# Past the head of the kernel, scales cross the partitions by a DMA transpose of 16-bit powers of two in SBUF instead of a float32 transpose on TensorE

## The chip, the cores and the metric

The kernel runs on one core of a Trainium2 chip. Five engines work from their own in-order queues: TensorE (PE, with its weight loads PEld), VectorE (DVE), ScalarE (ACT), GpSimd (POOL) and SyncE (SP), the last of which here does nothing but issue DMAs. The metric is the device time of one execution in microseconds (us); lower is better.

## The reference

Two independent parts are computed and set side by side. Part A is causal sliding-window attention with 32 heads of 32 columns and a window of 256; part B is a Fourier mixing layer as matrix products.

```python
# A: x [2048, 1024], wqkv [1024, 3072], wo [1024, 1024]
qkv = (x @ wqkv).reshape(B, S, 3, H, Dh)            # H = 32, Dh = 32
scores = einsum("bhqd,bhkd->bhqk", q, k) * Dh ** -0.5
mask = (i - j >= 0) & (i - j < 256)
a = softmax(where(mask, scores, -1e9)) @ v  ->  [S, D] @ wo
# B: x [2048, 1024], sequence DFT [2048, 2048] and hidden DFT [1024, 1024], real and imaginary
p = x @ hid_re.T ; r = x @ hid_im.T
b = seq_re @ p - seq_im @ r
out = concatenate([a, b], axis=-1)                   # [1, 2048, 2048] float32
```

## The kernel before, in words

Every large product runs in float16 on TensorE with each operand split into a high and a low part (`PASSES`: high by high, high by low, low by high). So each float32 piece has to be scaled into float16's range first. The scale is a power of two taken from the largest value of the whole piece (or, where ScalarE measures it, from the sums of absolute values of each partition). Three steps make it:

- `top` (VectorE) or `mean` and `u_top` (ScalarE, output `junk`) leave one number per partition;
- `spread` reduces these to one column `[128, 1]`, called `top_u`, `top_wk` and so on;
- `scale_of` brings the 128 numbers of that column to every partition. Before the change TensorE transposes the column, broadcast to 128x128, against the identity `ident` into a PSUM tile `pt_...`; VectorE takes the maximum along each row of `pt`, masks its exponent, clamps it and takes the reciprocal.

The program has three stages. In the **head** (steps 0 to 10 of `order`) inputs arrive and the first scales are made. In the **projection stage** (96 steps; q, k and v of the heads, 24 matmuls of 512 columns each) a step `at(n, ...)` emits the loads, scales and splits that later steps need. In the **unit stage** 48 units follow: for each half of the DFT, 4 units of kind `x` (part B's first product) and 8 units of kind `c` (its second product). A unit is seven sub-products of 12 matmuls (function `seven`), at positions 0 to 6 in three PSUM banks in the order a, b, a, c, a, b, a. At position 4 bank a is added into the output tile by VectorE (`y<-p_a`, line 1035), at position 5 bank b is (`y<-p_b`). Position 6 accumulates into bank a again, so it can't begin before the add of position 4 has read the bank.

Attention (`attention`) is a generator that `tick` advances in small steps between the matmuls of both stages. Its blocks need VectorE (masking `s`, maximum `mx`, low part `hl`, sum `o`), ScalarE, GpSimd and a DMA transpose from SP for each block (`t<-hl`, 128x512 or 128x1024 of float16) and one for each four blocks (`ot<-ohl`, 128x512).

For a unit of kind `c` the hooks are, counted from its own number n: load its two raw pieces `raw_u` in unit n - 3, measure them (`u_top`) at positions 0 and 2 of unit n - 2, `u_scale` at position 6 of unit n - 2, split (`un_a`, `un_b`, `un_c`) in unit n - 1. This is only the order in which the code is written. A list scheduler with its own model of each operation's time decides in which order each engine's queue holds the instructions, within what data and explicit `issue_after` edges allow.

Of the kernel before, what the change touches and what calls it, by code (L numbers as in the profile page):

```python
# [9 lines left out]
F32 = mybir.dt.float32  # L10
F32R = mybir.dt.float32r
F16 = mybir.dt.float16
BF16 = mybir.dt.bfloat16
U8 = mybir.dt.uint8
U32 = mybir.dt.uint32
AF = mybir.ActivationFunctionType
ALU = mybir.AluOpType
AX = mybir.AxisListType

P = 128  # L20
S = 2048
D = 1024
H = 32
# [5 lines left out]
CH = 512  # L29
NCH = S // CH  # L30
QB = CH // P
VW = 2 * DH + 2
# [8 lines left out]
VW = 2 * DH + 2  # L41
# [12 lines left out]
def fused_kernel(ctx: ExitStack, tc: tile.TileContext, xa, wqk, wv, wo, xb, wd, cs, out):  # L54
    nc = tc.nc
# [8 lines left out]
    const = ctx.enter_context(tc.tile_pool(name="const", bufs=1))  # L64
# [4 lines left out]
    ps_v = ctx.enter_context(tc.tile_pool(name="ps_v", bufs=1, space=PSUM))  # L69
# [8 lines left out]
    tsum = reg1[:, :7 * 8 * CH].rearrange("p (s h k c) -> p s h k c", s=7, h=2, k=4)  # L78
    spare = reg1[:, 7 * 8 * CH:]

    ident = const.tile([P, P], F32, name="ident")
    make_identity(nc, ident)


    upper = const.tile([P, P], F32, name="upper")
# [2 lines left out]
                            fill=0.0, base=0, pattern=[[1, P]], channel_multiplier=-1)  # L88
    upper2 = upper.bitcast(U32).unsqueeze(1).to_broadcast([P, 2, P])
    never = const.tile([P, 1], F32, name="never")  # L90
# [3 lines left out]
    pshift = const.tile([P, 1], F32, name="pshift")  # L94
    nc.gpsimd.memset(pshift, PSHIFT)

    nbank, units_on = [0], []

    def bank(name):
        nbank[0] += 1  # L100
        return ps_m.tile([P, CH], F32, tag=f"m{nbank[0] % 3}", name=name)
# [6 lines left out]

    junk = const.tile([P, ND * P], U8, name="junk")
    fixed = []  # L110
# [8 lines left out]
    def vec(f, *args, **kwargs):  # L119
        with tc.issue_after(latest[0].ins) if strict[0] and latest else nullcontext():  # L120
            latest[:] = [f(*args, **kwargs)]  # L121
        return latest[0]
# [10 lines left out]
        return const.tile([P, 2], F32, name=f"sc_{name}")  # L133

    tops, head = {}, [True]


    behind = []
# [18 lines left out]
    def spread(key, n):  # L157
        t = tops.pop(key)
        if n > 1:
            t1 = small.tile([P, 1], F32, tag="top0", name=f"top1_{key}")  # L160
            vec(nc.vector.tensor_reduce, t1, t, axis=AX.X, op=ALU.max)
        else:
            t1 = t
        tops[key] = t1

    def scale_of(key, v, s, down=2.0 ** -14):

        if head[0]:
            pt = ps_s.tile([P, CH], F32, tag="s", name=f"pt_{key}")[:, :P]
            with tc.issue_after(fixed[0].ins) if fixed else nullcontext():  # L170
                fixed[:] = [nc.tensor.transpose(pt, tops.pop(key).to_broadcast([P, P]), ident)]
        else:
            pt = (ps_v.tile([P, CH], F32, tag="pv", name=f"pt_{key}") if units_on else bank(f"pt_{key}"))[:, :P]
            nc.tensor.transpose(pt, tops.pop(key).to_broadcast([P, P]), ident)
        vec(nc.vector.tensor_reduce, v, pt, axis=AX.X, op=ALU.max)
        vec(nc.vector.tensor_scalar, v.bitcast(U32), v.bitcast(U32), 0x7F800000, None, op0=ALU.bitwise_and)
        vec(nc.vector.tensor_scalar, v, v, 2.0 ** -100, down, op0=ALU.max, op1=ALU.mult)
        vec(nc.vector.reciprocal, s, v)
# [218 lines left out]
    def at(n, f, *args):  # L397
        tasks.setdefault(n, []).append((f, args))
# [151 lines left out]
    for (kd, g), n in use.items():  # L550
        if kd in "qk" and n >= 4:
            at(n - 6, w_load, kd, g)
            at(n - 4, w_top, kd, g)
            at(n - 3, w_finish, kd, g)
    for g in range(NG):
        at(max(use["q", g], use["k", g], 11), scores_scale, g)

# [3 lines left out]
        at(n, x_split, 0, (i,), behind_act)  # L561
    at(7, strict.__setitem__, 0, False)
    at(7, head.__setitem__, 0, False)
    at(4, x_top, 2, (0, 1))
    at(5, x_top, 2, (2, 3))
    at(7, x_finish, 2)
# [4 lines left out]
    at(11, x_known)  # L571
    at(11, wv_load, 0)
    at(14, wv_top, 0)
    at(15, wv_scale, 0)
    for i, n in enumerate((15, 16, 16, 17)):
        at(n, wv_split, 0, (i,))
    at(15, wv_load, 1)
    at(18, wv_top, 1)
    at(19, wv_scale, 1)
    for i, n in enumerate((19, 20, 21, 21)):  # L580
        at(n, wv_split, 1, (i,))
    at(20, wv_known)
    def scan(key, ns):
# [292 lines left out]
    at(len(order) - 3, x_left, 0, "c")  # L876


    with tc.tile_pool(name="pa", bufs=2) as pa:
        def qk_out(kd, g, c, ps, f):  # L880
            y = pa.tile([P, 2, CH], F16, tag="yq", name=f"y{kd}{g}_{c}")
            behind_act[:] = [nc.scalar.activation(y[:, 0], ps, AF.Copy, scale=f)]
            behind[:] = [vec(nc.vector.scalar_tensor_tensor, y[:, 1], ps, f, y[:, 0],
                             op0=ALU.mult, op1=ALU.subtract)]
            a = "qk".index(kd)
            nc.sync.dma_start(qk[g, c, a:a + 2, :, :, a].rearrange("j d h t -> (d h) j t"), y)
            nc.sync.dma_start(qk[g, c, 2 - 2 * a, :, :, a].rearrange("d h t -> (d h) t"), y[:, 0])

        def d_out(g):
            qk_out("q", g, 0, direct.pop(g), f0[:, g:g + 1])  # L890

        w_top("q", 0)
        x_top(0, (0, 1, 2, 3))
        d_mm(0, range(0, 4))
        w_scale("q", 0)
        d_mm(0, range(4, 8))
        w_top("q", 1)
        d_mm(1, range(0, 1))
        x_scale(0)
        d_known(0)  # L900
        d_mm(1, range(1, 3))
        w_scale("q", 1)
        d_known(1)
        d_out(0)
        w_split("q", 0)
        w_top("q", 2)
        d_mm(1, range(3, 8))
        x_top(1, (0, 1))
        d_out(1)
        d_mm(2, range(0, 2))  # L910
        w_scale("q", 2)
        d_known(2)
        x_top(1, (2, 3))
        d_mm(2, range(2, 8))
        w_top("q", 3)
        d_mm(3, range(0, 2))
        x_scale(1)
        x_split(1, (0, 1))
        d_out(2)
        d_mm(3, range(2, 4))  # L920
        w_scale("q", 3)
        d_known(3)
        x_split(1, (2,))
        d_mm(3, range(4, 8))
        x_split(1, (3,))
        w_split("q", 1)
        d_out(3)

        for n, (kd, g, c) in enumerate(order):
            if n < 4:  # L930
                continue
            if n == 22:
                first_cm.__exit__(None, None, None)
                att_cm = tc.tile_pool(name="att", bufs=2, side="right")
                cell["att"] = att_cm.__enter__()
                agen[0] = attention()
                upcoming[0] = next(agen[0])
            for f, args in tasks.pop(n, ()):
                f(*args)
            rate[0] = 2 * early * EARLY.get(n, 0.85) / 24  # L940
            ps = bank(f"p{kd}{g}_{c}")
            if kd == "v":
                t = c
                product(ps, lambda h, d: xin[:, t // 4, h, d, t % 4 * P:t % 4 * P + P],
                        lambda h, d: reg2[:, g, h, d])
                y = pa.tile([P, H // 2, VW], F16, tag="yv", name=f"yv{g}_{t}")
                nc.gpsimd.memset(y[:, :, DH:DH + 1], 1.0)
                nc.gpsimd.memset(y[:, :, 2 * DH + 1:], 0.0)
                f = vf[:, g, t // 4:t // 4 + 1]
                pv = ps.rearrange("p (h d) -> p h d", d=DH)  # L950
                behind_act[:] = [nc.scalar.activation(y[:, :, :DH], pv, AF.Copy, scale=f)]
                behind[:] = [nc.vector.scalar_tensor_tensor(y[:, :, DH + 1:2 * DH + 1], pv, f, y[:, :, :DH],
                                                            op0=ALU.mult, op1=ALU.subtract)]
                nc.sync.dma_start(vs[t, :, g * (H // 2) * VW:(g + 1) * (H // 2) * VW],
                                  y.rearrange("p h w -> p (h w)"))
            else:
                u = wun[kd, g]
                product(ps, lambda h, d: u[:, h, d], lambda h, d: xin[:, c, h, d])
                qk_out(kd, g, c, ps, DOWN if kd == "q" else kf[:, c:c + 1])
            if kd == "v" and g == 0 and c % 4 == 3:  # L960
                ready.add((0, c // 4))
            if kd == "v" and g == 1 and c == NT - 1:
                pass
            if kd == "k" and g > 0:
                ready.add((g, c))
# [116 lines left out]
            hook(pos)  # L1082


    units_on.append(True)
    perm, turns = [(nbank[0] + 1 + k) % 3 for k in range(3)], [0]
    with tc.tile_pool(name="pb", bufs=1) as pb:
        ybufs = [pb.tile([P, 2, CH], F32, name=f"y{k}") for k in range(3)]
        ybufs.append(spare[:, 16 * P:].bitcast(F32).rearrange("p (e c) -> p e c", e=2))
        ny = [0]  # L1090
# [11 lines left out]
        for r in range(4):  # L1102
            x0, c0 = 12 * r, 12 * r + 4
            for j in range(4):
                n = x0 + j
# [5 lines left out]
            for j in range(8):  # L1111
                n = c0 + j
# [20 lines left out]
        for n, (kind, p, c, i) in enumerate(units):  # L1133
# [35 lines left out]
            f = fu.pop(n)  # L1169
# [16 lines left out]
        for q in range(NT // 2):  # L1186
# [5 lines left out]
                  lambda t, y, at_=0: nc.sync.dma_start(out[t * P:t * P + P, at_:at_ + y.shape[1] * y.shape[2]],  # L1192
                                                        y.rearrange("p e c -> p (e c)")),
# [51 lines left out]
```

## Time and profile before

| what | us |
|---|---|
| runs of the kernel before, median of 3 | 1716.21 (1709.82 to 1716.93) |
| the profiled execution, whole | 1715.44 |
| its span, first to last instruction | 1713.7 |
| DVE busy in the span | 1302.1 |
| ACT busy | 1170.1 |
| POOL busy | 575.5 |

The profile gives, for each engine, busy time and the idle time ahead of a group of instructions with what ended it. A wait for several things is put down to the one that came last. Matmuls overlap one another, so the distance from one matmul's start to the next, not its duration, is what it takes of TensorE. The 1.7 us between span and whole execution lie outside the first and last instruction.

### The profile page before, as it was taken

The page shows a single profiled execution, that of the slowest core. Times are in us where ns is not written, and L with a number is a line of the kernel's source. Part 1 is how long each engine was busy: PE and PEld are TensorE (multiplying, and loading weights), DVE is VectorE, ACT ScalarE, POOL GpSimd, SP SyncE. Part 2 cuts the span into 40 slices and gives each one's busy share as a digit, 9 for nine tenths or more (in the row PEclk, how much of TensorE's full clock was granted, in tenths as well). Part 3 has the DMA queues.
Part 4 walks back from the last instruction along what each step waited for, and adds up shares of the span by engine and source line. Part 5 has one row for each costly group of instructions (what it writes and reads, how often), then busy time and mean ns, then how long its engine had stood idle before and what let it go on. Part 6 is the DMA issues. An engine that isn't in the chain of part 4 may idle for free.

```text
span 1713.7 us, 30874 instructions
## 1 busy us (share of the span) xinstructions
PE 1694.8 (99%) x10999; PEld 852.4 (50%) x10999; DVE 1302.1 (76%) x2225; ACT 1170.1 (68%) x2035; POOL 575.5 (34%) x874
## 2 busy tenths in 40 slices
PE   9999999999999999999999999999999989999999
PEld 4444555555555544555554555545545545444444
DVE  6847788887987788887688886698876698688442
ACT  4566666676877787887687886688876678563322
POOL 0001222344434441444423565434565424411000
PEclk9999999999999999999999999999999999999999
DMA  9747999999998994887998999987999986875431
GB/s 349 245 137 242 252 291 289 271 262 299 243 245 198 215 226 121 206 196 182 229 244 241 196 182 181 223 196 127 197 169 185 203 203 127 166 193 118 117 98 74
DMA packets 469899, 348.63 MB, mean 203 GB/s; under 512 B 376944, under 2 KB 409968, under 8 KB 468848
## 3 DMA queue, kind: packets, MB, share of 16 engines
q1 hardware_dynamic: 462064, 321.48, 74.7%
q0 software_dynamic: 7680, 25.17, 9.2%
q8 instruction: 86, 1.41, 0.4%
q14 instruction: 69, 0.57, 0.1%
HBM read 166.99 MB, written 106.17 MB: 159 GB/s over the span
## 4 chain that ended last, share of the span: by engine, by line
PE 84%; DMA 5%; DVE 4%; ACT 4%; issue 2%; POOL 1%; SPq 0%; ACTq 0%; DVEq 0%; POOLq 0%
PE p_a L114 23%; PE pv L114 14%; PE p_b L114 11%; PE pk L114 9%; PE pq L114 9%; PE p_c L114 6%; PE po_a L114 5%; PE s L114 3%; PE po_b L114 2%; DMA raw_u<-in_cs_dram 2%; DMA t<-hl 1%; PE far L114 1%; PE po_c L114 1%; ACT reg L833 1%; DVE raw_u L791 1%
## 5 line engine op out<-in xcount | busy, mean ns | idle before, releaser
L266 ACT ACTIVATE s<-s,bias,escs 128x256 f32<-128x256 f32 (+1 forms) x512 | 270.1, 528 | 11.7
L284 POOL TENSOR_SCALAR_AFFINE_SELECT z<-t 128x512 f16<-128x512 f16 x224 | 186.4, 840 | 180.4 <-PE pv L114 137.4
L270 DVE TENSOR_TENSOR hl<-s,hl 128x512 f16<-128x512 f32 (+1 forms) x256 | 169.9, 664 | 61.6 <-ACT hl L269 59.5
L259 ACT ACTIVATE bias<-mx,pshift,escs 128x2 f32<-128x2 f32 x256 | 98.2, 384 | 169.3 <-DVE mx L256 168.8
L114 PEld LDWEIGHTS <-reg 128*128 128x128 f16 x1344 | 129.1, 98 | 141.5
L286 POOL TENSOR_SCALAR_AFFINE_SELECT t<-t 128x512 f16<-128x512 f16 x224 | 183.9, 830 | 11.4
L114 PE MATMUL p_a<-reg,un_c 128*128 128x512 f16 x768 | 181.2, 379 | 1.8 <-ACT y L1033 1.3
L114 PE MATMUL pk<-reg,wu_k 128*128 128x512 f16 x768 | 174.4, 379 | 0.0
L256 DVE TENSOR_REDUCE mx<-s 128x2 f32<-128x512 f32 (+1 forms) x256 | 170.7, 667 | 3.4
L114 PE MATMUL pv<-reg,reg 128*128 128x512 f16 x768 | 172.7, 379 | 0.0
L114 PEld LDWEIGHTS <-un_c 128*128 128x128 f16 x1152 | 110.0, 97 | 124.0 <-issue 4.9
L114 PEld LDWEIGHTS <-un_b 128*128 128x128 f16 x1152 | 110.1, 97 | 123.9 <-issue 7.8
L263 POOL TENSOR_SCALAR mark<-bias 128x1 f32<-128x1 f32 x128 | 52.3, 409 | 355.2 <-ACT bias L259 355.0
L114 PEld LDWEIGHTS <-un_a 128*128 128x128 f16 x1152 | 109.8, 97 | 116.2
L269 ACT ACTIVATE hl<-s 128x512 f16<-128x512 f32 (+1 forms) x256 | 148.8, 581 | 13.6 <-DMA t<-hl 8.3
L114 PE MATMUL pq<-reg,wu_q 128*128 128x512 f16 x672 | 151.3, 379 | 0.8 <-DVE reg L121 0.5
L114 PE MATMUL p_a<-reg,un_b 128*128 128x512 f16 x576 | 136.4, 379 | 4.7 <-DVE y L1035 3.0
L114 PE MATMUL p_b<-reg,un_b 128*128 128x512 f16 x576 | 136.3, 379 | 1.2 <-ACT y L1033 1.0
L114 PE MATMUL p_a<-reg,un_a 128*128 128x512 f16 x576 | 136.6, 379 | 0.0
L114 PE MATMUL p_c<-reg,un_a 128*128 128x512 f16 x576 | 136.5, 379 | 0.0
L254 DVE COPY_PREDICATED s<-upper,far 128x256 f32<-128x256 uint32 x224 | 94.2, 420 | 46.0 <-PE s L114 45.0
L114 PEld LDWEIGHTS <-qk 96*128 96x128 f16 x1056 | 87.9, 97 | 64.1 <-DMA qk<-qk 1.9
(208 smaller groups left out, 3154.1 us busy)
## 6 DMA issues: line engine op xcount, KB each, us to landing
raw_u<-in_cs_dram SPq DMA_DIRECT2D x64, 512.0 KB, 4.9
qk<-qk SPq DMA_DIRECT2D x64, 384.0 KB, 5.1
out_dram<-y POOLq DMA_DIRECT2D x72, 256.0 KB, 6.3
raw_wd<-in_wd_dram SPq DMA_DIRECT2D x24, 512.0 KB, 5.3
vs<-yv SPq DMA_DIRECT2D x32, 264.0 KB, 4.2
vt<-vs SPq DMA_DIRECT2D x64, 132.0 KB, 4.2
raw_wo<-in_wo_dram SPq DMA_DIRECT2D x16, 512.0 KB, 9.2
qk<-yq SPq DMA_DIRECT2D x32, 256.0 KB, 3.1
```

Source lines behind the costliest of these rows:

```text
L114: fixed[:] = [nc.tensor.matmul(*args, **kwargs)]
L254: nc.vector.copy_predicated(s[:, :, P:], upper2, d["far"] if nb == 3 else never2)
L256: nc.vector.tensor_reduce(mx, sv, axis=AX.X, op=ALU.max, negate=True)
L259: nc.scalar.activation(bias, mx, AF.Identity, bias=pshift, scale=es)
L263: marks[:] = [nc.gpsimd.tensor_scalar(mark, bias[:, 0:1], 1.0, None, op0=ALU.mult)]
L266: nc.scalar.activation(sv[:, h], sv[:, h], AF.Exp, bias=bias[:, h:h + 1], scale=es)
L269: nc.scalar.activation(hi, sv, AF.Copy)
L270: behind[:] = [nc.vector.tensor_tensor(lo, sv, hi, op=ALU.subtract)]
L284: nc.gpsimd.affine_select(out=z, in_=pk, compare_op=ALU.is_gt, fill=0.0, base=0, pattern=[[0, 4], [-1, P]], channel_multiplier=1)
L286: nc.gpsimd.affine_select(out=pk, in_=pk, compare_op=ALU.is_ge, fill=0.0, base=0, pattern=[[0, 4], [1, P]], channel_multiplier=-1)
L791: nc.vector.tensor_tensor(o, a, b, op=op)
L833: nc.scalar.activation(hi, src, AF.Copy)
```

## The change

From step 11 of the projection stage on, `spread` itself sends the column across. VectorE writes the upper 16 bits of the float32 column, masked to the exponent, 128 times side by side into `pb` (128x128 of 16 bits, an exact power of two read as bfloat16). SP issues a DMA transpose from `pb` to `pc`, both in SBUF. `scale_of` then reduces `pc` instead of a PSUM tile, without the masking operation. The head keeps the old way. The tiles `pb` and `pc` lie in the pool of the running stage (three buffers in the projection stage, one in the unit stage). `ident` moves into the end of `reg1` (overwritten by the last x split, after its last use), and the output tiles of q, k and v share one tag of three buffers instead of two tags of two. The weights' scale and split (`w_finish`) are written one step later, likewise `wv_scale` and `wv_split`. `u_scale` stays at position 6.

```diff
-    ident = const.tile([P, P], F32, name="ident")
+    ident = spare[:, :2 * P].bitcast(F32)
...
     tops, head = {}, [True]
+    crossing, crossed = [None], {}
...
         tops[key] = t1
+        if crossing[0]:
+            pb = crossing[0].tile([P, P], F16, tag="pb", name=f"pb_{key}")
+            nc.vector.tensor_scalar(pb.bitcast(U16), t1.bitcast(U16)[:, 1:2].to_broadcast([P, P]), 0x7F80, None,
+                                    op0=ALU.bitwise_and)
+            pc = crossing[0].tile([P, 1, P], F16, tag="pc", name=f"pc_{key}")
+            nc.sync.dma_start_transpose(pc, pb)
+            crossed[key] = pc.rearrange("p a t -> p (a t)").bitcast(BF16)
 
     def scale_of(key, v, s, down=2.0 ** -14):
 
+        if key in crossed:
+            nc.vector.tensor_reduce(v, crossed.pop(key), axis=AX.X, op=ALU.max)
+            nc.vector.tensor_scalar(v, v, 2.0 ** -100, down, op0=ALU.max, op1=ALU.mult)
+            nc.vector.reciprocal(s, v)
+            return
...
-            pt = (ps_v.tile([P, CH], F32, tag="pv", name=f"pt_{key}") if units_on else bank(f"pt_{key}"))[:, :P]
+            pt = bank(f"pt_{key}")[:, :P]
...
-            at(n - 3, w_finish, kd, g)
+            at(n - 3 if n < 16 else n - 2, w_finish, kd, g)
...
+    at(11, lambda: crossing.__setitem__(0, pa))
...
-    at(15, wv_scale, 0)
-    for i, n in enumerate((15, 16, 16, 17)):
+    at(16, wv_scale, 0)
+    for i, n in enumerate((16, 17, 17, 18)):
...
-    at(19, wv_scale, 1)
-    for i, n in enumerate((19, 20, 21, 21)):
+    at(20, wv_scale, 1)
+    for i, n in enumerate((20, 21, 21, 22)):
...
-    with tc.tile_pool(name="pa", bufs=2) as pa:
+    with tc.tile_pool(name="pa", bufs=3) as pa:
         def qk_out(kd, g, c, ps, f):
-            y = pa.tile([P, 2, CH], F16, tag="yq", name=f"y{kd}{g}_{c}")
+            y = pa.tile([P, 2, CH], F16, tag="y", name=f"y{kd}{g}_{c}")
...
-                y = pa.tile([P, H // 2, VW], F16, tag="yv", name=f"yv{g}_{t}")
+                y = pa.tile([P, H // 2, VW], F16, tag="y", name=f"yv{g}_{t}")
...
-    units_on.append(True)
...
     with tc.tile_pool(name="pb", bufs=1) as pb:
+        crossing[0] = pb
```

On TensorE's queue the 57 transposes `pt` of the steps from 11 on are gone and every other instruction keeps its place. What moves is seen on VectorE and SP. The place shown is unit 18 of the unit stage, while the scale of unit 20 is made. First VectorE's queue before the change, from the column `top_u` to the reduction of its transpose `pt_u` (the last row); `y<-p_18_a` is the add of position 4, `y<-p_18_b` that of position 5.

```order
L121 TENSOR_REDUCE top_u_11936<-top_u_11845 128x1
L270 TENSOR_TENSOR hl_11907<-s_11893,hl_11907 128x512
L318 TENSOR_REDUCE o_1_2_11853<-pv_11974 128x132
L327 RECIPROCAL rs_1_2_12000<-o_1_2_11853 128x8
L121 SCALAR_TENSOR_TENSOR un_c<-raw_u_1_11353,sc_u_11799,un_c 128x1024
L270 TENSOR_TENSOR hl_11953<-s_11943,hl_11953 128x256
L1035 SCALAR_TENSOR_TENSOR y_6765<-p_18_a,fu_11520,y_6765 128x512
L254 COPY_PREDICATED s_12022<-upper,never 128x2x128
L121 SCALAR_TENSOR_TENSOR un_b<-raw_u_0_11479,sc_u_11799,un_b 128x1024
L256 TENSOR_REDUCE mx_12026<-s_12022 128x2
L1035 SCALAR_TENSOR_TENSOR y_6765<-p_18_b,fu_11520,y_6765 128x512
L121 TENSOR_REDUCE sc_u_12093<-pt_u_12094 128x1
```

The same place of VectorE's queue after the change.

```order
L123 TENSOR_REDUCE top_u_11972<-top_u_11881 128x1
L170 TENSOR_SCALAR pb_u_11974<-top_u_11972 128x128
L285 TENSOR_TENSOR hl_11943<-s_11929,hl_11943 128x512
L179 TENSOR_REDUCE sc_u_12133<-pc_u_11976 128x1
L333 TENSOR_REDUCE o_1_2_11889<-pv_12014 128x132
L180 TENSOR_SCALAR sc_u_12133<-sc_u_12133 128x1
L342 RECIPROCAL rs_1_2_12040<-o_1_2_11889 128x8
L181 RECIPROCAL sc_u_12133<-sc_u_12133 128x1
L787 TENSOR_SCALAR fu_12137<-fa,sc_u_12133 128x1
L123 SCALAR_TENSOR_TENSOR un_c<-raw_u_1_11387,sc_u_11838,un_c 128x1024
L285 TENSOR_TENSOR hl_11993<-s_11983,hl_11993 128x256
L1051 SCALAR_TENSOR_TENSOR y_6789<-p_18_a,fu_11555,y_6789 128x512
```

The reduction that needs the crossing has moved from behind both adds to a place two rows behind `pb_u`, ahead of both adds. SP's queue at the same place, before the change:

```order
L272 DMA_TRANSPOSE t_11777<-hl_11774 128x8x128
L222 DMA qk_0_1_12052<-qk 96x2048
L272 DMA_TRANSPOSE t_11831<-hl_11828 128x8x128
L272 DMA_TRANSPOSE t_11910<-hl_11907 128x8x128
L752 DMA raw_u_0_12061<-in_cs_dram 128x1024
```

and after it:

```order
L287 DMA_TRANSPOSE t_11816<-hl_11813 128x8x128
L287 DMA_TRANSPOSE t_11867<-hl_11864 128x8x128
L237 DMA qk_0_1_12092<-qk 96x2048
L173 DMA_TRANSPOSE pc_u_11976<-pb_u_11974 128x1x128
L287 DMA_TRANSPOSE t_11946<-hl_11943 128x8x128
L768 DMA raw_u_0_12101<-in_cs_dram 128x1024
```

One more DMA transpose stands between the two of attention's blocks, and one of those has changed places with the load `qk`.

More of the change, by code (lines that the diff above doesn't have):

```diff
@@ L14 @@
 U8 = mybir.dt.uint8
+U16 = mybir.dt.uint16
 U32 = mybir.dt.uint32
@@ L95, in fused_kernel @@
     nc.gpsimd.memset(pshift, PSHIFT)
-    nbank, units_on = [0], []
+    nbank = [0]
     def bank(name):
```

## The prediction

> **What bounds the kernel now.** I read the page first, then the waits, then windows of the unit stage, then the timeline around single scales.
>
> ```profile
> PE 1694.8 (99%) x10999; PEld 852.4 (50%) x10999; DVE 1302.1 (76%) x2225; ACT 1170.1 (68%) x2035; POOL 575.5 (34%) x874
> ...
> PE 84%; DMA 5%; DVE 4%; ACT 4%; issue 2%; POOL 1%; SPq 0%; ACTq 0%; DVEq 0%; POOLq 0%
> ...
> L114 PE MATMUL pk<-reg,wu_k 128*128 128x512 f16 x768 | 174.4, 379 | 0.0
> ```
>
> TensorE is busy for 1694.8 of 1713.7 us and holds 84% of the chain that ended last. So whatever leaves its queue is gained in full, and whatever makes it wait is paid in full. In the projection stage it waits for nobody: 768 matmuls `pk` without idle time ahead of them. In the unit stage the page is less comfortable:
>
> ```profile
> PE p_a L114 <- DVE y L1035: 4.4, 6, 1.7
> ```
>
> Six times TensorE stood still because VectorE had not yet done an add `y<-p_...`. These columns are the sum, the times and the longest wait. VectorE is also the busiest engine behind TensorE there:
>
> ```profile
> 870.00:1030.00 160.00, 157.33 (x1080) 80.41 (x1079) 137.82 (x248) 128.11 (x231) 71.25 (x95) 1.00 0.97 214
> 1120.00:1290.00 170.00, 167.93 (x1181) 86.81 (x1179) 145.13 (x263) 138.02 (x249) 81.00 (x108) 1.00 0.91 168
> ```
>
> The columns are stretch, length, then busy time of PE, PEld, DVE, ACT, POOL. VectorE works 137.82 of 160 us and 145.13 of 170, that is 86% and 85%. The clock column is 1.00, so throttling plays no part.
>
> **What the removed transposes cost.** Two rows give the price of one on TensorE:
>
> ```profile
> 631.49 0.27 PE L174 MATMUL pt_u<-ident,top_u 128*128 128x128 f32 x1
> ...
> 631.60 1.89 PE L114 MATMUL p_a<-reg,un_a 128*128 128x512 f16 x8
> ```
>
> ```profile
> L174 PE MATMUL pt_u<-ident,top_u 128*128 128x128 f32 x32 | 8.8, 274 | 0.6 <-DVE o L318 0.6
> ...
> L174 PE MATMUL pt_wk<-ident,top_wk 128*128 128x128 f32 x8 | 2.2, 273 | 0.0
> L174 PE MATMUL pt_xp<-ident,top_xp 128*128 128x128 f32 x8 | 2.2, 273 | 0.0
> ...
> L174 PE MATMUL pt_wq<-ident,top_wq 128*128 128x128 f32 x4 | 1.1, 280 | 0.0
> ```
>
> The transpose starts at 631.49 and the next matmul at 631.60: it takes 0.11 us of TensorE's time, though its own record lasts 0.27. The change takes 57 of them away: 32 for the units of kind c, 8 for k's weights, 8 for part B's input, 4 for q's, and 5 single ones for `wv`, `wo` and `wd`. 57 x 0.11 = **6.3 us gained** for certain. The PSUM banks that they no longer use I put at nothing: the column of idle time shows 0.6 us in all ahead of `pt_u` and 0.0 ahead of the others (bounds: 0 to 2 us gained).
>
> **What the new operations cost by themselves.** VectorE gets a `pb` write of 128x128 elements for each scale and loses a masking operation on one column. The nearest rows:
>
> ```profile
> L254 DVE COPY_PREDICATED_SCALAR s<-upper,never 128x256 f32 x32 | 15.2, 477 | 5.9 <-PE s L114 5.9
> ...
> L121 DVE TENSOR_SCALAR sc_u<-sc_u 128x1 uint32<-128x1 uint32 x64 | 9.6, 149 | 1.2
> ...
> L121 DVE TENSOR_REDUCE sc_u<-pt_u 128x1 f32<-128x128 f32 x32 | 9.0, 282 | 8.2 <-PE pt_u L174 8.2
> ```
>
> A column costs 149 ns, 256 float32 elements of a row 477 ns; `pb` lies between, and I take 200, nearer the column because the elements are half as wide. The reduction of `pc` I leave at the 282 ns of the one of `pt_u` (not below 149). That is 57 x (0.20 - 0.15), about 3 us on VectorE, hidden under TensorE if it delays no add. The transposes move 57 x 32 KB = 1.9 MB, little beside the 64 transposes `ot` of 128 KB (8.4 MB) and the larger ones of `t`. Freed buffers (the shared tag), the identity's new place and the later steps of `w_finish` and `wv_split` touch engines that TensorE doesn't wait for in the projection stage (0.0 above): nothing, bounds -1 to +3 us.
>
> **The wait.** It decides. The place shown in the section on the change is typical of the unit stage: before, the reduction of `pt_u` stood behind both adds of its unit; now the reduction of `pc_u` stands 1 to 5 rows behind `pb_u` and, in 29 of 32 units, ahead of the add of position 4. VectorE's queue is in order, so until the DMA has landed nothing behind it runs: the sum `o`, the splits, then the add that TensorE needs for position 6. How long does a transposing DMA take here?
>
> ```profile
> L335 SPq DMA_TRANSPOSE ot<-ohl x64: 1188/1213/2481, 194.3 to 1486.7; - x64
> ...
> DMA to landing us min/median/max: 1.7/3.8/10.4
> ...
> L272 SPq DMA_TRANSPOSE t<-hl x256: 1188/1293/7147, 150.8 to 1468.7; - x128
> ...
> DMA to landing us min/median/max: 2.3/4.8/14.8
> ```
>
> SP is held 1.2 us by either size (min/median/max in ns), and `ot`, four tiles of 128x128, lands 1.7 us after issue at best and 3.8 at the median. One tile should come a little below: I take 3.0, between 1.7 and 3.8. With 0.2 for `pb` and 0.4 for SP (its queue has a `t<-hl` just ahead) the crossing is there 3.6 us behind `top_u`; bounds 2.0 (nothing queued, best landing) and 5.5 (another transpose's 1.2 ahead, the median of `ot`).
>
> The rows that the scheduler set between `pb` and the reduction fill 1.7 us on average (0.2 to 4.0, each row at its group's mean). So VectorE would wait 3.6 - 0.2 - 1.7, or about 1.7 us, a unit. One row says that this scheduler does place consumers too close behind such a DMA:
>
> ```profile
> SPq L354 <- DMA ot<-ohl: 134.9, 58, 9.1
> ```
>
> 58 of 64 times SP stood waiting for `ot` to land, 134.9 / 58 = 2.3 us each.
>
> **What a VectorE wait costs at this place.** The trace has two accidents of this kind. The first, around 957 us, is at the very rows listed in the change, the second at 1247 us in unit 32:
>
> ```profile
> 957.20 0.14 DVE L121 TENSOR_REDUCE top_u<-top_u 128x1 f32<-128x2 f32 x1
> 958.21 0.69 DVE L270 TENSOR_TENSOR hl<-s,hl 128x512 f16<-128x512 f32 x1 [0.88 <-ACT hl L269]
> ...
> 960.18 1.28 DVE L121 SCALAR_TENSOR_TENSOR un_c<-raw_u,sc_u,un_c 128x1024 f16<-128x1024 f32 x1 [0.69 <-ACT un_c L127]
> ...
> 961.71 0.74 DVE L1035 SCALAR_TENSOR_TENSOR y<-p_a,fu,y 128x512 f32<-128x512 f32 x1
> ...
> 962.50 1.89 PE L114 MATMUL p_a<-reg,un_b 128*128 128x512 f16 x8 [0.90 <-DVE y L1035]
> ```
>
> ```profile
> 1251.96 0.69 DVE L270 TENSOR_TENSOR hl<-s,hl 128x512 f16<-128x512 f32 x1 [4.41 <-ACT hl L269]
> ...
> 1253.85 1.28 DVE L121 SCALAR_TENSOR_TENSOR un_c<-raw_u,sc_u,un_c 128x1024 f16<-128x1024 f32 x1 [0.86 <-ACT un_c L127]
> ...
> 1255.16 0.70 DVE L1035 SCALAR_TENSOR_TENSOR y<-p_a,fu,y 128x512 f32<-128x512 f32 x1
> ...
> 1255.92 1.89 PE L114 MATMUL p_a<-reg,un_b 128*128 128x512 f16 x8 [1.70 <-DVE y L1035]
> ```
>
> Idle VectorE time of 0.88 + 0.69 = 1.57 us made TensorE wait 0.90; 4.41 + 0.86 = 5.27 made it wait 1.70. So 0.57 and 0.32 us for each us. How much the other units forgive is the distance from the end of the add to position 6. First and last of the 32:
>
> ```profile
> 625.11 0.74 DVE L1035 SCALAR_TENSOR_TENSOR y<-p_a,fx,y 128x512 f32<-128x512 f32 x1
> ...
> 627.81 1.89 PE L114 MATMUL p_a<-wx,un_c 128*128 128x512 f16 x8
> ...
> 1523.87 0.74 DVE L1035 SCALAR_TENSOR_TENSOR y<-p_a,fu,y 128x512 f32<-128x512 f32 x1
> ...
> 1525.68 1.67 PE L114 MATMUL p_a<-reg,un_b 128*128 128x512 f16 x7
> ```
>
> 627.81 - 625.85 = 1.96 us, and 1525.68 - 1524.61 = 1.07. Over all 32 the distances run from 0.01 to 2.4 us, 0.87 on average, and nine are under 0.1: there every late add is paid at once.
>
> The add also has four small rows more ahead of it than before (the reduction 0.28, the clamp 0.15, the reciprocal 0.16, `fu` 0.19: 0.8 us). A unit's delay is 1.7 + 0.8 = 2.5 us, less what VectorE idles here anyway (0.9 at the median of the 32 units; 1.57 in the first accident above, nothing in the last unit), less the distance of 0.87: 0.73 us. Over 29 units that is 21 us. By the two accidents it is 29 x 1.7 = 49 us of VectorE waiting at 0.32 to 0.57, or 16 to 28. Taking the landing from both sides moves it: a crossing 2.5 us behind `top_u` leaves about 8 us, one at 4.5 us about 43. I take **21 us lost**. The 25 crossings of the projection stage should make VectorE wait as long, but an output bank there has a whole later product of 24 matmuls before it is needed again: nothing, bounds 0 to 5.
>
> Sum, against the profiled execution's 1715.4: 1715.4 - 6.3 + 21 = **1730 us**. That execution lies 0.8 us below the median of the runs, well inside their 7 us spread.
>
> **A rule weighed.** The Trainium skill (VectorE: DVE Perf Modes, "The three transpose paths" and "Rules for kernel authors") speaks against this change: for 128x128 it puts the TensorE way at 390 ns and the DMA way at 1309 ns, and advises TensorE where PSUM will do. The trace's slot on TensorE is 0.11 us and its fastest four-tile DMA 1.7. If the page's 1309 ns held here as a landing time, the crossing would arrive about 1.9 us behind `top_u`, and the estimate by it would be 1715.4 - 6.3 + 3 = 1712 us; the first rival below has that outcome.
>
> **The rivals.**
> - *The wait is covered.* The crossing lands while VectorE does the 1.7 us of rows in between, and its other idle time takes the rest. For: `ot` can land in 1.7 us with four times the bytes; 14% of VectorE's time is idle. Against: 58 waits of 2.3 us on SP. It holds where the crossing is there within about 2.3 us of `top_u`. Time 1715.4 - 6.3 + 0 to 5 = 1709 to 1714.
> - *Faster than that.* The freed PSUM banks and the scale being ready earlier (the reduction now stands ahead of `y<-p_18_b`, not behind) take away some of TensorE's waits for VectorE too, 4.4 us in all: 1715.4 - 6.3 - 4.4 = 1705. Against: the same row makes the adds later.
> - *Worse.* Landings like the longest above (10.4 and 14.8 us) or SP stuck ahead of `pc` behind a store of `ot` put the crossing at 4.5 us or more: 1715.4 - 6.3 + 43 = 1752.
> - *It doesn't do what it says.* TensorE's queue shows 57 transposes fewer, so this one is out.
>
> **How the numbers follow.** Forecast (the crossing there 2.5 to 4.5 us behind `top_u`, 1716 to 1745): 0.52. Covered: 0.27. Faster: 0.08. Worse: 0.13. The likeliest gives 1730, own range 1716 to 1745. The whole range goes from 1707, which leaves out the faster case, to 1748, which leaves out most of the worse one. About 0.5% (8.6 us) is what a measurement of this kernel can tell from no change: faster means below 1707.6, slower above 1724.8. Faster takes the 0.08 and a little of the covered case, 0.09; the rest of the covered case and the lower third of the forecast are no change, 0.42; what remains is slower, 0.49.
>
> **What would show it.** No `pt` rows from the projection stage on, and 57 rows `pc<-pb` on SP. In VectorE's waits a row `sc_u <- DMA pc_u` with some 30 waits of 1 to 3 us where `sc_u <- PE pt_u` stood. TensorE's row `p_a <- DVE y` grown from 4.4 us to 20 or more: if the first is there and the second is not, the slack was larger than I read it, and the time is near 1710. If `pc` lands within 1.5 us of its issue, the step on the landing is wrong. If TensorE waits in the projection stage, the cover there was wrong.

## The result, and the profile after

| | before | after |
|---|---|---|
| device time, median | 1714.89 us | 1803.23 us |
| range of the runs | 1709.82 to 1718.91 (6) | 1790.48 to 1807.31 (6) |
| profiled execution, span | 1715.4, 1713.7 us | 1790.48, 1788.1 us |
| mean granted clock of TensorE | 1.000 | 0.991 |

The ratio is 1.0509, with a 95% interval of 1.0475 to 1.0542: **5% slower**, on the side that the prediction held likeliest, but far above its 1730 us and above its range. First the page of after: busy time, the shares of the chain that ended last, and two of TensorE's groups (count, busy time and mean ns of one, then the idle time ahead of them and what ended most of it).

```profile
PE 1708.5 (96%) x10942; PEld 847.9 (47%) x10942; DVE 1305.2 (73%) x2225; ACT 1167.3 (65%) x2035; POOL 567.5 (32%) x874
...
PE 50%; DVE 20%; DMA 12%; ACT 8%; issue 7%; POOL 1%; SPq 1%; DVEq 0%; ACTq 0%; POOLq 0%
...
L116 PE MATMUL p_a<-reg,un_b 128*128 128x512 f16 x576 | 144.2, 395 | 34.5 <-DVE y L1051 26.8
L116 PE MATMUL pk<-reg,wu_k 128*128 128x512 f16 x768 | 176.4, 383 | 0.0
```

TensorE has 57 matmuls fewer and holds only half of the chain, where it held 84%. VectorE went from 4% to 20%, the DMAs from 5% to 12%. Where the time was lost is read from the same matmuls in both traces. The start of a matmul early in the unit stage and of one behind its last loss, before:

```profile
597.47 1.03 PE L114 MATMUL p_c<-reg,un_a 128*128 128x512 f16 x4
...
1530.86 2.75 PE L114 MATMUL p_b<-reg,un_b 128*128 128x512 f16 x12
```

and after:

```profile
622.56 1.03 PE L116 MATMUL p_c<-reg,un_a 128*128 128x512 f16 x4
...
1605.31 2.75 PE L116 MATMUL p_b<-reg,un_b 128*128 128x512 f16 x12
```

The lag is 622.56 - 597.47 = 25.1 us when the projection stage has ended, and 1605.31 - 1530.86 = 74.5 us at the end of the unit stage; behind it nothing is added. With the transposes that TensorE no longer does (25 and 32 of 0.11 us) the two stages lost 27.8 and 52.9 us in this execution. The first figure is net of some 1.3 us by which TensorE was ahead here when the head ended (the lag of the same matmuls at 76 us), so the projection stage itself lost about 29. TensorE's waits (sum, times, longest, us):

```profile
PE p_a L116 <- DVE y L1051: 31.3, 22, 4.4
PE far L116 <- DVE s L269: 17.2, 13, 3.4
PE p_a L116 <- ACT p_c L1083: 11.3, 7, 5.0
```

The first row was 4.4 us in 6 waits. The second is attention's: `far` and `s` are its two score tiles in PSUM, and their next product waits until VectorE has joined them (`COPY_PREDICATED s<-upper,far`, line 269). The third comes over ScalarE, whose copies `p_c` stand in one queue with its work for attention:

```profile
ACT bias L274 <- DVE mx L271: 217.0, 137, 7.9
```

ScalarE waits for attention's maximum `mx`, which VectorE makes, 217.0 us in all; before it was 168.8. VectorE's own waits in the view of waits after:

```profile
DVE sc_u L179 <- DMA pc_u<-pb_u: 75.8, 29, 6.7
DVE scw L179 <- DMA pc_wk<-pb_wk: 20.9, 8, 5.7
DVE vxp L179 <- DMA pc_xp<-pb_xp: 15.7, 7, 5.1
DVE scw L179 <- DMA pc_wq<-pb_wq: 12.0, 4, 5.4
```

Some 130 us of VectorE standing still in front of reductions whose DMA had not landed, 76 of them in the unit stage. The DMAs themselves (duration of an issue on SP in ns, minimum/median/maximum; then issue to landing in us), from the view of the tile `pc_u`:

```profile
L173 SPq DMA_TRANSPOSE pc_u<-pb_u x32: 1119/1162/2941, 648.1 to 1595.2; - x32
...
DMA to landing us min/median/max: 2.2/3.3/9.8
```

One place of each stage shows how a wait travels. The unit stage, in the timeline of after (start, duration, engine, row; in brackets the idle time ahead of it and what ended that):

```profile
1043.60 1.98 SPq L287 DMA_TRANSPOSE t<-hl  x1
...
1044.08 0.23 DVE L170 TENSOR_SCALAR pb_u<-top_u 128x128 uint16<-128x128 uint16 x1
...
1045.67 1.50 SPq L173 DMA_TRANSPOSE pc_u<-pb_u  x1
...
1050.71 0.29 DVE L179 TENSOR_REDUCE sc_u<-pc_u 128x1 f32<-128x128 bf16 x1 [6.41 <-DMA pc_u<-pb_u]
...
1052.50 0.74 DVE L1051 SCALAR_TENSOR_TENSOR y<-p_a,fu,y 128x512 f32<-128x512 f32 x1
...
1053.30 1.02 PE L116 MATMUL p_a<-reg,un_b 128*128 128x512 f16 x4 [3.35 <-DVE y L1051]
```

SP is still issuing a `t<-hl` when `pb_u` is ready, so the crossing starts 1.4 us late; it lands 5 us after that; VectorE stands for 6.41 us with the add of position 4 behind it in its queue; TensorE stands for 3.35. And the projection stage, same view:

```profile
471.62 0.28 DVE L179 TENSOR_REDUCE scw<-pc_wq 128x1 f32<-128x128 bf16 x1 [5.35 <-DMA pc_wq<-pb_wq]
...
472.01 0.42 DVE L269 COPY_PREDICATED s<-upper,far 128x256 f32<-128x256 uint32 x1
...
472.48 0.22 PE L116 MATMUL far<-qk,qk 96*128 96x128 f16 x1 [1.67 <-DVE s L269]
```

What waits behind the reduction here is no output bank but attention's row. The group `pk` still shows 0.0 of idle time, because the product that stands first in line when TensorE has to wait is always one of attention's.

Last the clock. Stretches of 3.41 us around one such gap, in the view of windows (columns: stretch, length, then busy time of PE, PEld, DVE, ACT, POOL; the first of the last three columns is the granted clock):

```profile
386.23:389.64 3.41, 3.41 (x19) 1.59 (x17) 1.11 (x3) 3.20 (x6) 0.62 (x1) 1.00 0.44 146
389.64:393.05 3.41, 1.53 (x11) 0.78 (x9) 3.38 (x8) 1.53 (x2) 0.62 (x1) 1.00 0.90 240
393.05:396.46 3.41, 3.41 (x32) 1.81 (x31) 3.41 (x5) 2.29 (x5) 2.84 (x3) 0.50 0.93 241
```

After a stretch in which TensorE worked 1.53 of 3.41 us, the next runs at half the clock. That happens eight times in after, 30.7 us in all, and not once between the start and the end of the profiled execution of before. By the spacing of the matmuls in those stretches it costs 13.6 us, which is part of the 27.8 and 52.9 above. The runs of after differ with the clock in part: the fastest, at 0.991, took 1790.48 us, the longest, at 0.982, 1807.31. But the gaps ahead of the half clock cost time themselves, and a run of 1799.40 us at 0.990 lies 9 us above the fastest, so how much of the spread is the clock's stays open.

### The profile page after: what moved, and what is told of

It reads as the page before. It is cut to its first block, busy times and chain, and to the rows that moved or that the text cites. A ratio compares the mean times of both kernels' runs of the same rounds, so it can differ in the third digit from the quotient of the medians.

```text
span 1788.1 us, 30909 instructions
## 1 busy us (share of the span) xinstructions
PE 1708.5 (96%) x10942; PEld 847.9 (47%) x10942; DVE 1305.2 (73%) x2225; ACT 1167.3 (65%) x2035; POOL 567.5 (32%) x874
## 4 chain that ended last, share of the span: by engine, by line
PE 50%; DVE 20%; DMA 12%; ACT 8%; issue 7%; POOL 1%; SPq 1%; DVEq 0%; ACTq 0%; POOLq 0%
PE p_a L116 16%; PE p_b L116 7%; PE pv L116 6%; PE pq L116 5%; DMA pc_u<-pb_u 5%; PE po_a L116 5%; PE p_c L116 4%; PE pk L116 3%; DVE mx L271 2%; PE po_b L116 2%; DVE hl L285 2%; ACT s L281 2%; DVE reg L850 2%; DVE raw_u L807 2%; DVE s L269 1%
## 5 line engine op out<-in xcount | busy, mean ns | idle before, releaser
L274 ACT ACTIVATE bias<-mx,pshift,escs 128x2 f32<-128x2 f32 x256 | 98.2, 384 | 217.4 <-DVE mx L271 217.0
L299 POOL TENSOR_SCALAR_AFFINE_SELECT z<-t 128x512 f16<-128x512 f16 x224 | 180.2, 831 | 134.2 <-PE pv L116 119.3
L301 POOL TENSOR_SCALAR_AFFINE_SELECT t<-t 128x512 f16<-128x512 f16 x224 | 190.5, 871 | 10.5
L116 PE MATMUL p_a<-reg,un_b 128*128 128x512 f16 x576 | 144.2, 395 | 34.5 <-DVE y L1051 26.8
```

The lines of the kernel that those rows point to most:

```text
L116: fixed[:] = [nc.tensor.matmul(*args, **kwargs)]
L274: nc.scalar.activation(bias, mx, AF.Identity, bias=pshift, scale=es)
L299: nc.gpsimd.affine_select(out=z, in_=pk, compare_op=ALU.is_gt, fill=0.0, base=0, pattern=[[0, 4], [-1, P]], channel_multiplier=1)
L301: nc.gpsimd.affine_select(out=pk, in_=pk, compare_op=ALU.is_ge, fill=0.0, base=0, pattern=[[0, 4], [1, P]], channel_multiplier=-1)
```

## The experiments

My theory was that the loss is VectorE's in-order queue: the reduction stands where its DMA has not landed, and rows that TensorE needs stand behind it. The rival was the 57 DMAs themselves: SP's queue, which they hold for 1.2 us each, and the collisions there.

**1. The reduction further back (`late`).** It is held behind the latest of the adds, evictions and attention rows that were written before it (the list `behind`).

```diff
-            nc.vector.tensor_reduce(v, crossed.pop(key), axis=AX.X, op=ALU.max)
+            with tc.issue_after(behind[0].ins):
+                nc.vector.tensor_reduce(v, crossed.pop(key), axis=AX.X, op=ALU.max)
```

> The reduction of pc is held behind the latest add or eviction of VectorE (in the unit stage behind the add of position 5); the DMA, its place on SP and all else stay. If the cost is VectorE standing in its in-order queue for a crossing that has not landed: VectorE's waits for pc fall from some 130 us to under 15, TensorE's gaps go back to those of the kernel before, the granted clock to 1.000, and the time is 1715 - 6 = 1709 us, within 4. If the cost is the 57 extra DMAs on SP and the DMA engines: about 1790 us, as the changed kernel.

Measured: 1730.78 us against 1714.21, ratio 1.0092 (1.006 to 1.0124). All 57 DMAs are there and most of the loss is gone, so the place of the reduction carried it. Not all: the 1709 us expected were missed, and some 16 us above the kernel before stay. One view of VectorE's waits, one of TensorE's and one place in the timeline say where a good part of them is:

```profile
DVE sc_u L180 <- DMA pc_u<-pb_u: 14.1, 2, 12.3
```

```profile
PE p_a L116 <- ACT p_c L1084: 12.7, 2, 10.9
```

```profile
1508.91 3.74 SPq L224 DMA_DIRECT2D raw_wo<-in_wo_dram  x8
...
1512.74 1.45 SPq L173 DMA_TRANSPOSE pc_u<-pb_u  x1
...
1528.34 0.29 DVE L180 TENSOR_REDUCE sc_u<-pc_u 128x1 f32<-128x128 bf16 x1 [12.32 <-DMA pc_u<-pb_u]
```

29 waits became 2, but one of them is 12.3 us: a crossing issued behind eight loads of 512 KB landed 15.6 us after its issue. TensorE's wait of 10.9 us follows it, over ScalarE.

**2. One stage at a time (`late_u`, `late_p`).** The same edit only where the key is a unit's, or only where it is not.

```diff
+            with tc.issue_after(behind[0].ins) if key[0] == "u" else nullcontext():
```

> The same, for the scales of the unit stage alone; in the projection stage the reduction stays early. If VectorE's wait is the cost, only the projection stage's loss is left: the changed kernel lost 27 us between 230 and 600 us there, so about 1709 + 27 = 1736 us. If it is the DMAs: about 1790 us.

> The same, for the projection stage alone; in the unit stage the reduction stays early. If VectorE's wait is the cost, the unit stage's loss is left, 49 us plus the 3.5 us gained by its 32 removed transposes: about 1709 + 52 = 1761 us. If it is the DMAs: about 1790 us.

A single execution of each gave 1754.1 and 1776.9 us, 18 and 16 us above the expectations; these had been reckoned from 1709, and `late` itself had come out some 20 us above that. Each was then timed in several runs.

> The reduction held behind VectorE's latest add or eviction in the unit stage only; in the projection stage it stands as in the change. This time in rounds, to give the two stages' shares an interval. If the loss is VectorE's in-order wait in both stages and the stages add up: 1731 (held in both) plus the projection stage's share, which one look put at 18 to 23 us: 1749 to 1754. Rival (the loss is nearly all the unit stage's, as the prediction had it with the projection stage at nothing): 1731 to 1736.

> The reduction held back in the projection stage only; in the unit stage it stands as in the change. If the stages add up: 1731 plus the unit stage's share, which one look put at 41 to 46 us: 1772 to 1780. Rival (the prediction's size of 21 us for the unit stage): 1752.

Measured: 1753.28 us, ratio 1.0232 (1.018 to 1.0285), with the projection stage as in the change; 1775.55 us, ratio 1.035 (1.0307 to 1.0394), with the unit stage as in the change. Above `late` that is 1.4% or 24 us for the projection stage and 2.6% or 44 us for the unit stage (each to some 10 us); with `late`'s own 0.9% they add up to 4.9% of the change's 5.1%. TensorE's waits, with the reduction held back in the units only:

```profile
PE far L116 <- DVE s L270: 17.8, 12, 3.5
...
PE p_a L116 <- DVE y L1052: 6.3, 4, 4.4
```

and in the projection stage only:

```profile
PE p_a L116 <- DVE y L1052: 41.1, 21, 5.0
...
PE far L116 <- DVE s L270: 0.5, 2, 0.4
```

Each edit takes away the wait of its own stage: the one on attention's scores is the projection stage's, the one on the output's adds the unit stage's. The way over ScalarE is the unit stage's too: with the reduction held back there, ScalarE's wait for `mx` is 171.9 us again and TensorE's row `p_a <- ACT p_c` 2.2.

**3. No wait at all, with and without the DMA (`own`, `own_nodma`).** The reduction reads `pb`, the partition's own powers of two, so the result lacks the crossing.

```diff
-            crossed[key] = pc.rearrange("p a t -> p (a t)").bitcast(BF16)
+            crossed[key] = pb.bitcast(BF16)
```

> The reduction reads pb instead of pc, so each partition uses its own scale and the crossing is left out of the result; the DMA transpose is still issued, and nobody reads what it brings. If VectorE's wait is the cost: about 1709 us, within 6, with the reduction as early as in the changed kernel. If the DMAs are: about 1790 us. If the early place of the reduction alone (without any wait) delays the adds: 1715 to 1740 us.

> The changed kernel without the transposing DMA: the reduction reads the partition's own powers of two (this leaves the crossing between partitions out). Theory of SyncE's queue (the 57 transposes on SyncE delay loads and attention's stores that stand behind them, and this is what the kernel without a wait, 1718.5, still loses): 1709, within 3, that is before less the 57 transposes on TensorE. Rival (the DMAs cost nothing; the rest of the loss comes from the 0.23 us writes on VectorE and from chance gaps): the same as the kernel with the DMAs, 1716 to 1720.

> The kernel with the DMA issued and not waited for (the reduction reads the partition's own powers of two; this leaves the crossing out), timed in rounds this time, beside the one without the DMA. Theory of SyncE's queue: 1718, some 9 us above the one without the DMA. Rival: both within 3 us of each other.

Measured: 1718.52 us in a single execution with the DMA; in several runs 1715.81 with it (ratio 0.9994, 0.9973 to 1.0016) and 1711.18 without (0.9981, 0.996 to 1.0001). The single 1718.5 was on the high side. The DMAs cost 4.6 us by the medians, half of what the theory of SP's queue said and more than its rival, with intervals that overlap: a small cost is likely and not settled. In both the reduction stands ahead of the add of position 4 in all 32 units, and TensorE's waits for the add come to 5.0 and 3.1 us (4.4 before), so the early place alone doesn't delay the adds. The 1711.18 us, with no crossing of any kind, lie 3.5 us under the kernel before: by the medians the 6.3 us of the transposes don't come out in full, but the interval reaches from 6.9 us gained to nothing. TensorE's longest wait there:

```profile
PE s L116 <- DMA qk<-qk: 5.5, 1, 5.5
```

At that point, 408 us into the span, TensorE runs 3 us ahead of before, and waits for a load of `qk` that SP issues at 409.07, where before it issued it at 408.20: TensorE came earlier and the load didn't. 3.0 us ahead become 3.8 us behind, part of it in the stretch at half clock that follows.

**4. The other edits alone (`rest`).** Before, with the shared tag and the later steps of `w_finish`, `wv_scale` and `wv_split`, the scales through TensorE. The identity's new place is not among them.

```diff
-            at(n - 3, w_finish, kd, g)
+            at(n - 3 if n < 16 else n - 2, w_finish, kd, g)
...
-    with tc.tile_pool(name="pa", bufs=2) as pa:
+    with tc.tile_pool(name="pa", bufs=3) as pa:
```

> The kernel before with only the edits that make room for the crossing: one tag y with three buffers in place of yq and yv with two each, the finish of a weight one position later from position 16 on, the scales and splits of wv one position later. Every scale still crosses through TensorE. If these edits are neutral: 1714 us, within 4 of before. If a part of the loss of the projection stage comes from them (weights finished later, or a buffer that is waited for): 1720 to 1735.

Measured: 1714.0 us, ratio 0.9997 (0.9974 to 1.002): neutral, within 4 or 5 us.

**5. Two mendings of SP's order (`late2`).** On top of `late`, the loads of `wo` behind the crossing written last (`lastpc`), and the reductions of `wo`, `wd1` and `wd0` a position later.

```diff
-        at(ns[-1] + 3, scan_scale, key)
+        at(ns[-1] + 4, scan_scale, key)
...
+        def load_wo(dst, src):
+            with tc.issue_after(lastpc[0].ins):
+                line[:] = [nc.sync.dma_start(dst, src)]
...
-                            do(n + turn // 7, turn % 7, load, raw[k][b], wo[b % 2, 2 * (b // 2) + k])
+                            turn = max(turn, 3)
+                            do(n + turn // 7, turn % 7, load_wo, raw[k][b], wo[b % 2, 2 * (b // 2) + k])
```

> The kernel with the reduction behind VectorE's latest add or eviction, and two mendings of SyncE's order: the eight loads of wo behind the last two crossings that stand near them, and the three reductions of wo, wd1 and wd0 one position later. Theory of SyncE's queue: the two waits of 12.3 and 5.3 us of VectorE go, with them some 15 us of TensorE and the half clock behind them: 1712 to 1716, that is no slower than before. Rival (these waits only move to the next crossing or load in the queue): 1725 to 1731, as without the mendings. A result under 1706 would beat both kernels; I don't expect it.

Measured: 1723.09 us, ratio 1.0043 (1.0024 to 1.0062), some 8 us better than `late` and still slower than before; the expectation of 1712 to 1716 was missed. The two waits did go; for the units VectorE's view of waits has left

```profile
DVE sc_u L180 <- DMA pc_u<-pb_u: 2.3, 2, 1.9
```

and for the projection stage 2.6 us, but TensorE's has

```profile
PE p_a L116 <- DVE y L1052: 7.1, 6, 3.6
PE p_a L116 <- ACT y L1050: 5.9, 3, 4.9
PE s L116 <- DMA qk<-qk: 5.3, 1, 5.3
```

The last is the wait that also stands in the kernel without a crossing. The second hangs on GpSimd (ScalarE waited 5.28 us for attention's `o` there), and GpSimd on a DMA: it had waited 6.02 us for one of attention's transposes `t<-hl`. Why that one was late I didn't settle. The longest wait of each of the three rows goes with a stretch at half clock, 20.5 us in the whole execution.

**6. A longer crossing (`twice`).** A plain DMA copies `pc` back into `pb`, and the reduction reads it there.

```diff
-            crossed[key] = pc.rearrange("p a t -> p (a t)").bitcast(BF16)
+            nc.sync.dma_start(pb, pc.rearrange("p a t -> p (a t)"))
+            crossed[key] = pb.bitcast(BF16)
```

> The changed kernel with a crossing that is longer by one more hop: behind the transpose a plain DMA copies the 128x128 powers of two back into their first buffer, and the reduction, at its old place, reads them there. If the loss is VectorE's wait in front of the reduction, the 54 waits of about 2.4 us grow by the copy's way, 2.5 to 3.5 us each (estimate from the shortest landings, 2.2 us, and 0.5 us of issue), 135 to 190 us more of VectorE's wait, and at the 0.45 us of TensorE for each that the change showed, 60 to 85 us more: 1865 to 1890. Rival (the loss comes from a few collisions in SyncE's queue and from the half clock, not from the length of the wait): 57 more DMAs at 0.08 us each, as in the pair with and without the DMA, some 5 us: 1805 to 1815.

Measured: 1807.96 us, ratio 1.0548 (1.0506 to 1.059). That is the rival's number, and my theory's was 57 us and more above it. The reason is in the order of VectorE's program: the scheduler knows of the second hop and puts the reduction back by about as much. In the units it stands 6.7 rows behind `pb` on average, 3.0 in the change, and the add of position 4 stands ahead of it in 25 of 32 units, in the change in 3. VectorE's waits in front of the units' reductions, and TensorE's for the add, with the longer crossing:

```profile
DVE sc_u L180 <- DMA pb_u<-pc_u: 78.6, 25, 7.1
```

```profile
PE p_a L116 <- DVE y L1052: 15.1, 8, 5.6
PE p_b L116 <- ACT y L1050: 11.1, 7, 3.6
PE p_a L116 <- ACT p_c L1084: 11.0, 5, 5.7
```

The wait was hardly longer than in the change (75.8 us), so the run doesn't say what a longer one costs. It does say that the add is not all: the two matmuls that gave the lags above start at 629.02 and 1620.80 us here, so the unit stage lost 61.9 us, no less than the change's 52.9 (read from the fastest of its six runs), though TensorE's wait for the add is halved. 22 us of its waits are now for ScalarE's copies. To make the wait longer took a kernel in which the reduction can't move.

**7. The longer crossing, its reduction ahead of the adds (`twice_held`).** The unit's scale is written at position 3, and each add or eviction, those of the projection stage too, is held behind the latest reduction (the list `red`).

```diff
+    def behind_red(f, *args, **kwargs):
+        with tc.issue_after(red[0].ins) if red else nullcontext():
+            return f(*args, **kwargs)
...
-                do(n - 2, 6, u_scale, n)
+                do(n - 2, 3, u_scale, n)
```

> As the kernel with the longer crossing (1808.0 us), but in the unit stage the scheduler may not move the reduction behind the adds of the output tile: the scale is written at position 3 in place of 6, and every add or eviction that is written behind a reduction is held behind it. In the kernel with the longer crossing the a-add stood ahead of the reduction in 25 of 32 units (in the change in 3), which is why its waits grew so little; here it stands ahead in none. Theory of VectorE's wait: 1.5 to 2.8 us more of wait in each of 32 units, 48 to 90 us, at 0.45 to 0.7 us of TensorE each 22 to 63 us: 1830 to 1871. Rival (the length of the crossing doesn't count, only collisions in SyncE's queue and the half clock): the same as with the longer crossing, 1804 to 1812.

Measured: 1852.1 us, ratio 1.0779 (1.0719 to 1.0838), inside the theory's range, and yet not quite by its reasoning:

```profile
DVE sc_u L184 <- DMA pb_u<-pc_u: 84.4, 29, 8.0
```

```profile
PE p_a L116 <- DVE y L142: 75.1, 22, 8.9
```

```profile
core 0: 1853.9 us, clock 0.974
```

VectorE waits only 6 us more than in `twice`, where I expected 48 to 90; TensorE's wait for the add is five times as long, and the unit stage lost 103.4 us (the same two matmuls start at 637.45 and 1670.75). So the sum of VectorE's waits doesn't set what is paid; what stands behind them counts too. In `twice` that was mostly other rows, here it is always the add. And the clock takes part: 96 us at half clock here, 58 in `twice`, 31 in the change (without the last stretch of each). The edit reaches the projection stage as well, so the 44 us above `twice` are not all the units'.

## Why the prediction was wrong

**Right:** TensorE lost 57 transposes and nothing else; `pb` took 0.23 us (0.20 taken) and the reduction 286 ns (282 taken); the reduction stands ahead of the add of position 4 in 29 of 32 units and VectorE waits for the DMA in 29; the other edits are worth nothing that can be measured (`rest`); and the wait decides. Two of its own signs came true: the row `p_a <- DVE y` grew from 4.4 to 31.3 us, and TensorE waited in the projection stage, which was its sign that the cover there was wrong.

**The landing** was mis-sized a little. I took 3.6 us from `top_u` to the crossed row; from the start of `pb` it is 4.4 on average (0.23 for `pb`, 0.51 until SP issues, 3.66 from there to the reduction), within the bounds of 2.0 to 5.5. I put one tile below the median of the four-tile `ot`; in fact its 3.3 us median is near that of `ot`, 3.8. VectorE's wait came out at 75.8 / 32 = 2.4 us a unit, not 1.7. The Trainium skill (VectorE: DVE Perf Modes, "The three transpose paths") gives 1309 ns for this path; no landing here was under 2.2 us.

**The step that failed in the projection stage** is "an output bank there has a whole later product of 24 matmuls before it is needed again: nothing, bounds 0 to 5". True of the output banks, but TensorE's queue also carries attention's score products, whose two PSUM tiles were not free in time (17.2 us of waits), and the rows that free them stand behind the same reduction. It lost 27.8 us in the profile, 24 by the pair of `late` and `late_u_r`. The 0.0 us of idle time ahead of `pk` said that nothing was late, not that anything had slack.

**The term that was mis-sized in the unit stage** is the 21 us, where 52.9 were lost. Most of the difference is the longer crossing: the prediction's own prices gave 43 us at 4.5 us behind `top_u`, and 4.4 it was. The rest is the clock: six of the eight stretches at half clock lie in the unit stage and cost, by the spacing of their matmuls, some 9 us of the 52.9. Without them TensorE lost 0.57 us for each us that VectorE waited (43.5 / 75.8), the upper of the two accidents' 0.32 and 0.57. Reckoned in the same way it is 0.56 in `twice` (61.9 less some 18 of half clock, over 78.6) and 0.94 in `twice_held` (103.4 less some 24, over 84.4). So there is no fixed price: it rose where the add always stands behind the wait, and that an accident's price fitted the change is partly luck.

**The clock** I had set aside with "throttling plays no part", read from the stretches of before. It plays none as long as TensorE has no gaps; the gaps that the waits made brought 13.6 us with them in the profiled execution, and more in the median run, which lies 12.7 us above it at clocks of 0.985 to 0.989.

The sum with what was measured, on the profiled execution: 1715.4 - 6.3 + 27.8 + 52.9 = 1789.8, against 1790.5. It must close, since both losses were read from the same two traces as lags plus the transposes; it shows where the time went, not why. Of the rivals, "worse" had the right mechanism and nearly the right unit term, 43 us, with 1752 us and a chance of 0.13; what it lacked is the projection stage and the clock.

That no crossing by DMA can win here is not shown, only made likely: the kernel without any crossing is at 1711.2, and the best one with it at 1723.1. Issuing the crossings from another engine's queue wasn't tried.

## What to carry to other kernels

When a step on the bound engine gives way to a DMA, ask first what the step takes there (0.11 us here, 6.3 in all), then list everything that stands behind the DMA's consumer on its in-order engine, and who waits for each of those rows: all of the bound engine's products, not only the stage's main one. Where a scheduler sets the order by its own model, look at where it puts the consumer; one explicit edge behind the rows that the bound engine needs was worth 72 of the 88 us. And idle time of 0.0 ahead of a group says nothing of how much delay it would forgive.

## What was not expected of the hardware

**Half clock after short gaps.** In 13 profiled executions (after and the experiments, away from start and end) the granted clock fell to 0.50 for stretches that are whole multiples of 3.41 us, always right after such a stretch in which TensorE had stood idle for 2.04 us or more, 84 times. No stretch with over 2.2 us of idle time was spared, none under 2.04 was punished. Idle time is counted here from the end of a matmul's usual spacing to the next start; the stretch shown above, 1.88 us by its busy column, counts 2.04 so. The Trainium skill (TensorE: Matmul & The Clock Gate, its table of the two states) has the slow state come after an idle window of about 3.4 us; the window's length agrees with the trace, but six tenths of it idle were enough here. Shorter waits that fall into one stretch add up: in `twice`, two of 1.61 and 0.61 us brought the half clock at 801.8 us, and five of the 84 cases are of this kind.

**A small transpose is hardly cheaper to issue.** 128x128 elements hold SP for 1.16 us at the median and up to 2.94, nearly as long as the larger ones that the prediction shows (1.21 and 1.29); and behind eight loads of 512 KB one landed 15.6 us after its issue.
